# A fused attention and feed-forward kernel: the opening work of batches 0 and 1 is put in another order

## The chip, the cores and the metric

The kernel runs on one core of a Trainium2 chip. The metric is the device time of one execution in microseconds (us). Three executions of the kernel before took 340.25, 342.08 and 343.45 us, so their median is 342.08 us. Inputs and output are float32 in the chip's main memory; most arithmetic inside is float16, with float32 accumulation.

## The reference, cut to what matters

Eight batches of eight heads, 576 positions and 64 numbers per head go through an attention with two kinds of mask. The result is laid out as 4608 tokens of 512 numbers and goes through two matrix products with a leaky activation between them.

```python
scores = scale * np.matmul(q, k.transpose(0, 1, 3, 2))
rel = pos[:, None] - pos[None, :]
mask_local = (rel >= 0) & (rel < stride)                       # heads 0 to 3, stride 32
mask_strided = (rel >= 0) & (pos[None, :] % stride == pos[:, None] % stride)   # heads 4 to 7
scores = np.where(masks[None, :, :, :], scores, -1000000000.0)
attn = np.exp(scores - max);  attn = attn / sum(attn)
x = np.matmul(attn, v).transpose(0, 2, 1, 3).reshape(B * S, H * D)
h = x @ w_in                                                   # 512 -> 2048
g = np.maximum(h, 0.0) + alpha * np.minimum(h, 0.0)
out = g @ w_out                                                # 2048 -> 512
```

The kernel leaves out the subtraction of the maximum and gets each row's sum from a column of ones behind `v`.

## The kernel before, in words

Tokens are handled in nine chunks of 512. Layer 1 of a chunk makes `gT` (16 groups of 128 hidden units by 512 tokens): TensorE (PE) multiplies `win16` with the transposed attention result `xT`, ScalarE (ACT) writes the negative part into `neg`, VectorE (DVE) combines both into `gT`. Layer 2 multiplies `gT` with `wout16` and stores. Chunk 0 needs tokens 0 to 511 of batch 0; chunk 1 needs the last 64 tokens of batch 0 and most of batch 1.

Order is written out by hand. Every instruction goes through `keep`, so on each engine the instructions stand in the order in which the Python code issues them. An engine works its queue strictly in that order, and waits on semaphores where an input or a buffer isn't ready. The DMAs issued from GpSimd (POOL) stand in POOL's own queue among its copies and memsets; there are eight semaphores for them in turn, so each such DMA is issued only after the one eight places earlier has landed.

**Batch 0** is made in three parts of tokens (`pt` 0 and 1 with 256 tokens each, `pt` 2 with 64) by the functions named `dense_*`: `turn_s` and `turn_l` transpose q and k of the strided and of the local heads, `vcast` arranges v, `dense_s` and `dense_l` make scores and exponentials, `dense_pv` the weighted sums, `dense_x` the transposes into `xT`. In the kernel before, the first part runs alone; then layer 1 of chunk 0 starts on its tokens (`lin1_half(f, i)`: `f` is the half of the tokens, `i` one of eight pairs of hidden groups), the second part is put in as two blocks of five or six jobs after `lin1_half(0, 1)` and `lin1_half(0, 3)`, and the other twelve `lin1_half` follow without anything between them.

**Layer 2 of chunk 0** (L1181) is 48 matmuls of 512 columns: 16 values of `kf` for three banks of 128 tokens, in one run; the fourth group of tokens is made by four `lin2_piece` later. Then the third part of batch 0 runs, and then **batch 1** (`alone(3, 2)`): it has two units, 3 (the strided heads, pairs 6 and 7 of heads) and 2 (the local heads, pairs 4 and 5). `T(u, "q")` and `T(u, "k")` transpose a unit's q and k, `score_early` makes the scores of a pair and adds the mask to them by matmuls with an identity (L322), `Pv(g, a)` makes a third or a half of a pair's weighted sums, `X(g)` transposes them into `xT`. Chunk 1 starts after that (its first matmuls are those of L634), and from there on the attention of the next batch is put between the matmuls of a chunk.

**PSUM** has eight banks in three pools: `ps` (three one-bank buffers), `ph` (three, tag `hps`) and `pb` (one buffer of two banks, `sp`). The exponentials go to six buffers `et` in turn, 640 columns wide. The scores fill 576 of them. A `Pv` matmul takes 128 columns from its block's start, so that the last blocks also read columns 576 to 639, which are set to zero once (L1156, on DVE, between layer 1 and layer 2 of chunk 0).

**POOL's queue** is, in order: the loads of batch 0 and of `win16`; two tails, the last v rows of batch 0; four loads of `wout16` (`load_w(c, True)`); some memsets; unit 3 (`load_unit(1, True)`: q, k, tails, v) and unit 2 (`load_unit(1, False)`) of batch 1; q and k of batch 2's local heads (`load_qk`); the casts of batch 1 (`cast_v`, `cast_l`) and the copy `over_v` within v, with loads of batch 2 between and after them; `cast_l(2, ...)` last.

Of the kernel before, what the change touches and what calls it, by code (L numbers as in the profile page):

```python
# [41 lines left out]
def kernel(  # L42
# [10 lines left out]
    nc = tc.nc  # L53
# [333 lines left out]

    defer, defer_et = [], {}

    def score_both(P):  # L390

        w, r = P.w, 72 if P.strided else 128
        for i in range(2):
            et = ets[ectr["i"] % NE]
            ectr["i"] += 1
            if i:
                sps = [pspool.tile([128, 512], F32, tag="ps", name="sph") for _ in range(2)]
            else:
                sp = pbpool.tile([128, 2, 512], F32, tag="sp", name="sp")
                sps = [sp[:, y] for y in range(2)]  # L400
            grp = P.sgroups[i]
            n = w * len(grp)
            for x, t in enumerate(grp):
                if P.dx:
                    q0 = k0 = 80 * (4 * (2 * P.pr + t % 2) + t // 2)
                else:
                    q0, k0 = w * t, 32 + 72 * t if P.strided else 96 * t
                for y in range(2):
                    hf = slice(64 * y, 64 * y + 64)
                    keep(nc.tensor.matmul(  # L410
                        sps[y][:, w * x : w * x + w], P.kT[hf, k0 : k0 + 128],
                        P.qT[hf, q0 : q0 + w], start=(x == 0), stop=(x == len(grp) - 1),
                        skip_group_check=True))
                    P.et[(2 * (t // 2) + y, t % 2) if P.strided else (t, y)] = (et, n * y + w * x)
            ev = et[0:r, 0 : 2 * n]
            if not P.strided and i == 0:
                mv = ev.rearrange("r (y c) -> r y c", y=2)
                m = mfirst.unsqueeze(1).to_broadcast([r, 2, n])
            else:
                mv = ev.rearrange("r (c f) -> r c f", f=w)  # L420
                m = (mstr if P.strided else mother).unsqueeze(1).to_broadcast([r, 2 * n // w, w])
            if i == 0:
                keep(nc.scalar.activation(  # L423
                    ev.rearrange("r (y c) -> r y c", y=2), sp[0:r, :, 0:n], AF.Exp, scale=SCALE))
                keep(nc.gpsimd.tensor_tensor(mv, mv, m, op=ALU.mult))  # L425
# [487 lines left out]
    def dense_l(pt):  # L913

        b0, nb = 4 * pt, 4 if pt < 2 else 1
        nx = 2 if pt < 2 else 1
        sp = pbpool.tile([128, 2, 512], F32, tag="sp", name="sp")
        n = 192 * nx
        spv = sp[:, :, 0:n].rearrange("p e (y x c) -> p e y x c", y=2, x=nx)
        for e in range(2):  # L920
            fill(sp[:, e, 0:n], A["near"], 2 * nx, True)
        for e in range(2):
            hf = slice(64 * e, 64 * e + 64)
            for y in range(2):
                for kb in range(b0 - 1 if pt else 0, b0 + nb):
                    g = 64 * (kb % 2)
                    if kb < b0:
                        o, q0, w = spv[g : g + 64, e, y, nx - 1, 64:96], 64 * b0, 32
                    else:
                        w = 96 if kb < b0 + nb - 1 else 64  # L930
                        o, q0 = spv[g : g + 64, e, y, (kb - b0) // 2, 0:w], 64 * kb
# [3 lines left out]
        ed[("l", pt)] = [new_et()[:, 0:n] for _ in range(2)]  # L935
        for e in range(2):
            keep(nc.scalar.activation(ed[("l", pt)][e], sp[:, e, 0:n], AF.Exp, scale=SCALE))

    def dense_pv(kind, pt):

# [181 lines left out]
    dense_x("l", 0, "act")  # L1122
# [7 lines left out]
    keep(nc.vector.memset(qks["k"][64:80], 0.0))  # L1130
    keep(nc.vector.memset(x16s[64:80], 0.0))
    for i in range(2):
        keep(nc.gpsimd.memset(vls[i][0:32, 0:1, 0:64], 0.0))
        keep(nc.gpsimd.memset(vls[i][:, :, 64:65], 1.0))
        keep(nc.gpsimd.memset(vss[i][:, :, :, 64:65], 1.0))
    load_unit(1, True)
    load_unit(1, False)

    jobs = [
        lambda: turn_s("q", 1, "act"), lambda: turn_s("k", 1, "dve"),  # L1140
        lambda: dense_s(1), lambda: turn_l("q", 1, "act"), lambda: turn_l("k", 1, "dve"), lambda: vcast(1, "act"),
        lambda: dense_pv("s", 1), lambda: dense_l(1), lambda: dense_x("s", 1, ("act", "dve")),
        lambda: dense_pv("l", 1), lambda: dense_x("l", 1, "act")]
    for i in range(4):
        lin1_half(0, i)
        if i % 2:
            for _ in range(6):
                if jobs:
                    jobs.pop(0)()
    for f, i in ((1, 0), (1, 1), (1, 2), (1, 3), (0, 4), (0, 5), (1, 4), (1, 5), (0, 6), (0, 7), (1, 6), (1, 7)):  # L1150
        lin1_half(f, i)
    for i in range(2):
        keep(nc.vector.memset(kTs[i][:, :, 0:32], 0.0))
        keep(nc.vector.memset(kTs[i][:, :, 608:672], 0.0))
# [12 lines left out]
    load_d(2)  # L1167
    load_v(2, True)
# [3 lines left out]
    def attn_n(n, end):  # L1172
        for _ in range(n):
            attn_step(end)
        if n == 0:
            attn_step(0)

    banks = [phpool.tile([128, 512], F32, tag="hps", name="ops") for _ in range(3)]
    for kf in range(16):
        for mt in range(3):  # L1180
            keep(nc.tensor.matmul(  # L1181
                banks[mt], gTs[0][:, kf, 128 * mt : 128 * mt + 128], wout16[:, kf, :],
                start=(kf == 0), stop=(kf == 15)))
# [9 lines left out]
    dense_pv("s", 2)  # L1193
    dense_pv("l", 2)
    lin2_piece(0, 13)
    dense_x("s", 2, ("act", "dve"))
    dense_x("l", 2, "act")
    pos["i"] = end0
    for i in range(2):
        lin2_piece(0, 14 + i)  # L1200
        attn_step(end1)
        attn_step(end1)
    while pos["i"] < end1:
        attn_step(end1)
    wide["on"] = False
    load_unit(3, False)

# [58 lines left out]
```

## Time and profile before

| what | us |
|---|---|
| median of three executions | 342.08 |
| the profiled execution | 342.95 |
| its span, first to last instruction | 341.1 |
| opening, up to chunk 1's first matmul | 88.6 |
| chunks 1 to 8 | 252.5 |

The profile comes from one execution. It gives for each engine when an instruction ran, how long it was idle before it, and what ended that idle time. PEld is PE's loading of weights, which lies beside its matmuls. "PEclk" is the share of full clock that TensorE was granted. "L1181" is a line of the kernel before.

### The profile page before, as it was taken

The numbers are of one execution on the slowest core, as the hardware profiler recorded it, in microseconds if no ns is written. First come the engines' busy times: TensorE is split into PE (matmuls) and PEld (weight loads), VectorE is DVE, ScalarE is ACT, GpSimd is POOL, SyncE is SP. The second block draws the span as 40 slices with busy tenths as digits, with TensorE's granted clock in tenths as the row PEclk, the third lists the DMA queues.
The fourth block names the chain that finished last, engine by engine and source line by source line (L and its number), as shares of the span: only waits on it lengthen the run. The fifth ranks groups of instructions, "written<-read, shape, count | busy, mean of one in ns | idle before, by whom it ended". The sixth has DMA issues, their size and how long they took to land.

```text
span 341.1 us, 8353 instructions
## 1 busy us (share of the span) xinstructions
PE 317.3 (93%) x3436; PEld 211.0 (62%) x3436; DVE 219.7 (64%) x421; ACT 180.4 (53%) x335; POOL 174.3 (51%) x170
## 2 busy tenths in 40 slices
PE   8786989597899999999999999999999999999995
PEld 3564754356444544588778547854886776486484
DVE  3454561126578858875986689568847995864861
ACT  2242531126596557656755775577657626633740
POOL 7454577000359699749765774877372620400400
PEclk9787899969799999999999999999999999999999
DMA  8999999609904999749965992998071013003003
GB/s 188 210 201 206 237 170 114 143 1 213 197 1 54 137 161 234 95 67 208 206 67 98 258 153 25 160 152 98 19 171 50 20 32 112 0 2 126 0 2 123
DMA packets 81470, 40.18 MB, mean 118 GB/s; under 512 B 58440, under 2 KB 76728, under 8 KB 81432
## 3 DMA queue, kind: packets, MB, share of 16 engines
q0 software_dynamic: 41680, 16.76, 41.9%
q1 hardware_dynamic: 39608, 22.86, 29.3%
q8 instruction: 27, 0.44, 0.5%
q14 instruction: 11, 0.09, 0.1%
q10 hardware_dynamic: 144, 0.03, 0.0%
HBM read 38.15 MB, written 9.44 MB: 140 GB/s over the span
## 4 chain that ended last, share of the span: by engine, by line
PE 67%; DVE 15%; ACT 8%; issue 5%; DMA 2%; POOL 2%; SPq 0%; ACTq 0%; DVEq 0%
PE hps L634 23%; PE ops L761 19%; DVE gT L647 5%; PE hps L1059 5%; PE ops L675 4%; PE ops L1181 3%; DVE gsum L705 3%; PE pv L453 2%; ACT xT L492 2%; DVE x L462 2%; DMA madd_t<-consts 2%; ACT et L429 2%; PE sp L410 1%; ACT neg L644 1%; PE tp L250 1%
## 5 line engine op out<-in xcount | busy, mean ns | idle before, releaser
L634 PE MATMUL hps<-xT,win 128*128 128x512 f16 (+4 forms) x640 | 120.5, 339 | 0.6
L647 DVE SCALAR_TENSOR_TENSOR gT<-neg,oma,hps 128x512 f16<-128x512 f32 x128 | 93.6, 743 | 37.0 <-ACT neg L644 31.5
L644 ACT ACTIVATE neg<-hps 128x512 f32<-128x512 f32 x128 | 76.5, 598 | 35.5 <-PE hps L634 33.9
L634 PEld LDWEIGHTS <-win 128*128 128x128 f16 x640 | 56.9, 98 | 48.0 <-issue 3.2
L425 POOL TENSOR_TENSOR et<-et,consts 128x576 f16<-128x576 f16 (+1 forms) x24 | 30.7, 1278 | 58.4 <-ACT et L423 58.3
L705 POOL TENSOR_TENSOR gsum<-gT 128x1024 f16<-128x1024 f16 x14 | 29.7, 2129 | 40.5 <-DVE gT L647 40.5
L761 PEld LDWEIGHTS <-gsum 128*128 128x128 f16 x448 | 41.3, 98 | 7.6 <-DVE gsum L705 3.0
L761 PE MATMUL ops<-wsum,gsum 128*128 128x256 f16 x328 | 41.7, 273 | 1.0 <-DVE gsum L705 0.8
L761 PEld LDWEIGHTS <-gT 128*128 128x128 f16 x336 | 31.1, 98 | 6.8 <-DVE gT L647 1.6
L432 POOL TENSOR_TENSOR et<-et,consts 128x576 f16<-128x576 f16 (+1 forms) x24 | 30.9, 1286 | 0.6 <-ACT et L429 0.6
L761 PE MATMUL ops<-wout,gT 128*128 128x256 f16 x224 | 29.2, 273 | 0.5
L462 DVE TENSOR_TENSOR x<-pv,rc 96x384 f16<-96x384 f32 (+2 forms) x52 | 27.7, 533 | 1.8
L460 DVE RECIPROCAL rc<-pv 72x6 f32<-72x6 f32 (+2 forms) x70 | 12.8, 183 | 20.4 <-PE pv L453 20.3
L453 PEld LDWEIGHTS <-et 72*128 72x128 f16 (+1 forms) x392 | 20.6, 98 | 8.0 <-POOL et L432 0.8
L182 POOL DMA_DIRECT2D vl<-in_v_dram x7 | 10.1, 1437 | 28.1 <-PE pv L453 27.2
L423 ACT ACTIVATE et<-sp 128x576 f16<-128x576 f32 (+1 forms) x24 | 15.5, 646 | 12.9 <-PE sp L410 12.9
L675 PE MATMUL ops<-wout,gT 128*128 128x512 f16 x80 | 22.1, 404 | 0.0
L429 ACT ACTIVATE et<-sph 128x288 f16<-128x288 f32 (+1 forms) x48 | 18.4, 410 | 0.0
L1059 PE MATMUL hps<-xT,win 128*128 128x256 f16 x128 | 17.9, 302 | 0.5 <-ACT xT L190 0.5
L1067 DVE SCALAR_TENSOR_TENSOR gT<-neg,oma,hps 128x256 f16<-128x256 f32 x32 | 14.0, 478 | 6.6 <-ACT neg L1064 6.2
L778 ACT COPY par<-ops 128x512 f32<-128x512 f32 x13 | 7.6, 587 | 16.9 <-PE ops L761 16.9
L714 ACT COPY osb<-ops 128x512 f32<-128x512 f32 x14 | 8.2, 586 | 15.7 <-PE ops L761 15.7
(155 smaller groups left out, 423.6 us busy)
## 6 DMA issues: line engine op xcount, KB each, us to landing
out_dram<-osb SPq DMA_DIRECT2D x35, 256.0 KB, 3.0
ql<-in_q_dram SPq DMA_DIRECT2D x5, 512.0 KB, 4.1
kl<-in_k_dram SPq DMA_DIRECT2D x5, 512.0 KB, 6.9
vl<-in_v_dram POOLq DMA_DIRECT2D x6, 384.0 KB, 9.0
win<-in_moe_w_in_dram POOLq DMA_DIRECT2D x4, 512.0 KB, 10.8
wout<-in_moe_w_out_dram POOLq DMA_DIRECT2D x4, 512.0 KB, 12.9
stv<-in_v_dram POOLq DMA_DIRECT2D x7, 288.0 KB, 8.4
qsd<-in_q_dram POOLq DMA_DIRECT2D x6, 288.0 KB, 6.9
```

The costliest lines, as they stand in the source:

```text
L425: keep(nc.gpsimd.tensor_tensor(mv, mv, m, op=ALU.mult))
L429: keep(nc.scalar.activation(ev[:, n * y : n * y + n], sps[y][0:r, 0:n], AF.Exp, scale=SCALE))
L432: keep(nc.gpsimd.tensor_tensor(mv, mv, m, op=ALU.mult))
L453: keep(nc.tensor.matmul(pv[:, 65 * x : 65 * x + 65], et[0:r, c : c + 128], v16[0:r, 2 * P.pr + hh, t, :] if P.strided else v16[:, 6 * (2 * ...
L462: keep(nc.vector.tensor_tensor(P.x16[0:w, c0 : c0 + 64 * nb].rearrange("r (c e) -> r c e", e=64), pvv[:, :, 0:64], rc[0:w, 0:nb].unsqueeze ...
L634: keep(nc.tensor.matmul(hps[:, dst : dst + w], win16[:, kk, 128 * m : 128 * m + 128], xT[:, kk, src : src + w], start=(kk == 0 and x == 0) ...
L644: keep(nc.scalar.activation(neg, hps, AF.Relu, scale=-1.0))
L647: keep(nc.vector.scalar_tensor_tensor(gTs[n][:, m, :], neg, oma[:, m : m + 1], hps, op0=ALU.mult, op1=ALU.add))
L675: keep(nc.tensor.matmul(ops, gTs[n][:, kf, 128 * mt : 128 * mt + 128], wout16[:, kf, :], start=(kf == 0), stop=(kf == 15)))
L705: keep((nc.vector if eng == "dve" else nc.gpsimd).tensor_tensor(gsum[i][:, hs], a, b, op=op))
L761: keep(nc.tensor.matmul(o, lhs(y), rhs(y), start=(first and y == 0), stop=(y == 7), skip_group_check=True))
L1059: keep(nc.tensor.matmul(hps[:, 256 * j : 256 * j + 256], win16[:, kk, 128 * m : 128 * m + 128], xT[:, kk, 256 * f : 256 * f + 256], start= ...
```

## The change

- `score_both` gets a parameter `eng`. With it the mask is multiplied in after the exponentials by the engine named, with nothing put off; pairs 4 to 7 now use it with DVE, so that the mask matmuls of `score_early` go.
- `dense_l` takes one `ps` bank for each of its two halves in place of the two-bank buffer of `pb`.
- `turn_s` of the second part and `dense_s(1)` go in among the first part. The other eight jobs of the second part follow one by one behind the eight `lin1_half(0, i)`; the eight `lin1_half(1, i)` come after all of them.
- In layer 2 of chunk 0 the jobs of batch 1's strided heads (`T(3, ...)`, the scores and sums of pairs 6 and 7, `X(6)`) follow the values of `kf` from 5 on, one each. Batch 1's local heads are put between the third part of batch 0 and the four `lin2_piece`.
- Memsets go from DVE to POOL: those of `kT`, `qks` and `x16s` ahead of the loads of `wout16`, those of `et` behind `cast_l(2, ...)`.
- POOL loads the first two pieces of `wout16`, then unit 3, then the other two pieces, then unit 2, then the tails and last v rows of batch 0. `load_qk(2, ...)` comes behind the casts of batch 1.

```diff
-    def score_both(P):
+    def score_both(P, eng=None):
...
+            if eng is not None:
+                if i == 0:
+                    keep(nc.scalar.activation(
+                        ev.rearrange("r (y c) -> r y c", y=2), sp[0:r, :, 0:n], AF.Exp, scale=SCALE))
...
+                keep((nc.vector if eng == "dve" else nc.gpsimd).tensor_tensor(mv, mv, m, op=ALU.mult))
+                continue
...
-        sp = pbpool.tile([128, 2, 512], F32, tag="sp", name="sp")
...
         for e in range(2):
+            sp = pspool.tile([128, 512], F32, tag="ps", name="scl")
...
     dense_pv("s", 0)
+    turn_s("q", 1, "act")
     dense_l(0)
-    dense_x("s", 0, ("act", "dve"))
+    turn_s("k", 1, "act")
+    dense_x("s", 0, ("dve", "act"))
     dense_pv("l", 0)
...
+    dense_s(1)
+    dense_x("l", 0, "act")
...
-    load_tail(0, False)
-    first_vl(4, 64)
-    for c in range(4):
-        load_w(c, True)
-    keep(nc.vector.memset(qks["q"][64:80], 0.0))
...
+        keep(nc.gpsimd.memset(kTs[i][:, :, 608:672], 0.0))
+    for nm in "qk":
+        keep(nc.gpsimd.memset(qks[nm][64:80], 0.0))
+    keep(nc.gpsimd.memset(x16s[64:80], 0.0))
+    for c in range(2):
+        load_w(c, True)
     load_unit(1, True)
+    for c in range(2, 4):
+        load_w(c, True)
     load_unit(1, False)
+    load_tail(0, False)
+    first_vl(4, 64)
 
     jobs = [
...
+    for i in range(8):
         lin1_half(0, i)
+        jobs.pop(0)()
+    for i in range(8):
+        lin1_half(1, i)
...
-    for t in ets:
-        keep(nc.vector.memset(t[:, 576:640], 0.0))
-
-    load_qk(2, False, "q")
-    load_qk(2, False, "k")
     for pr in range(2):
         cast_v(1, pr, "pool")
     cast_l(1, "q")
-    load_tail(2, False)
     cast_l(1, "k")
     over_v(1, "pool")
+    load_qk(2, False, "q")
+    load_qk(2, False, "k")
+    load_tail(2, False)
     load_v(2, False)
     load_d(2)
     load_v(2, True)
     cast_l(2, "q")
     cast_l(2, "k")
...
+    jobs = [T(3, "q"), T(3, "k"), sc1(6), sc1(7), Pv(6, 0), Pv(6, 1), Pv(6, 2), Pv(7, 0), Pv(7, 1), X(6), Pv(7, 2)]
+    for t in ets:
+        keep(nc.gpsimd.memset(t[:, 576:640], 0.0))
     for kf in range(16):
         for mt in range(3):
             keep(nc.tensor.matmul(
                 banks[mt], gTs[0][:, kf, 128 * mt : 128 * mt + 128], wout16[:, kf, :],
                 start=(kf == 0), stop=(kf == 15)))
+        if kf >= 5:
+            jobs.pop(0)()
...
-    vcast(2, "dve")
-    rest_turn()
-    dense_s(2)
-    dense_l(2)
-    lin2_piece(0, 12)
...
+    jobs = [
+        T(2, "q"), T(2, "k"), X(7), lambda: lin2_piece(0, 12), sc1(4), rest_turn, sc1(5), lambda: lin2_piece(0, 13),
+        Pv(4, 0), Pv(4, 1), lambda: dense_s(2), lambda: vcast(2, "dve"), Pv(5, 0), X(4), lambda: dense_l(2),
+        Pv(5, 1), lambda: lin2_piece(0, 14), X(5),
+        lambda: dense_pv("s", 2), lambda: lin2_piece(0, 15), lambda: dense_pv("l", 2),
+        lambda: dense_x("s", 2, ("act", "dve")), lambda: dense_x("l", 2, "act")]
+    for fn in jobs:
+        fn()
```

More of the change, by code (lines that the diff above doesn't have):

```diff
@@ L421, in score_both @@
                 m = (mstr if P.strided else mother).unsqueeze(1).to_broadcast([r, 2 * n // w, w])
+            if eng is not None:
+                if i == 0:
+                    keep(nc.scalar.activation(
+                        ev.rearrange("r (y c) -> r y c", y=2), sp[0:r, :, 0:n], AF.Exp, scale=SCALE))
+                else:
+                    for y in range(2):
+                        keep(nc.scalar.activation(
+                            ev[:, n * y : n * y + n], sps[y][0:r, 0:n], AF.Exp, scale=SCALE))
+                keep((nc.vector if eng == "dve" else nc.gpsimd).tensor_tensor(mv, mv, m, op=ALU.mult))
+                continue
             if i == 0:
@@ L916, in dense_l @@
         nx = 2 if pt < 2 else 1
-        sp = pbpool.tile([128, 2, 512], F32, tag="sp", name="sp")
         n = 192 * nx
-        spv = sp[:, :, 0:n].rearrange("p e (y x c) -> p e y x c", y=2, x=nx)
+        ed[("l", pt)] = []
         for e in range(2):
-            fill(sp[:, e, 0:n], A["near"], 2 * nx, True)
-        for e in range(2):
+            sp = pspool.tile([128, 512], F32, tag="ps", name="scl")
+            spv = sp[:, 0:n].rearrange("p (y x c) -> p y x c", y=2, x=nx)
+            fill(sp[:, 0:n], A["near"], 2 * nx, True)
             hf = slice(64 * e, 64 * e + 64)
@@ L927, in dense_l @@
                     if kb < b0:
-                        o, q0, w = spv[g : g + 64, e, y, nx - 1, 64:96], 64 * b0, 32
+                        o, q0, w = spv[g : g + 64, y, nx - 1, 64:96], 64 * b0, 32
                     else:
                         w = 96 if kb < b0 + nb - 1 else 64
-                        o, q0 = spv[g : g + 64, e, y, (kb - b0) // 2, 0:w], 64 * kb
+                        o, q0 = spv[g : g + 64, y, (kb - b0) // 2, 0:w], 64 * kb
                     keep(nc.tensor.matmul(
@@ L934, in dense_l @@
                         start=False, stop=False, skip_group_check=True))
-        ed[("l", pt)] = [new_et()[:, 0:n] for _ in range(2)]
-        for e in range(2):
-            keep(nc.scalar.activation(ed[("l", pt)][e], sp[:, e, 0:n], AF.Exp, scale=SCALE))
+            et = new_et()[:, 0:n]
+            ed[("l", pt)].append(et)
+            keep(nc.scalar.activation(et, sp[:, 0:n], AF.Exp, scale=SCALE))
     def dense_pv(kind, pt):
@@ L1135 @@
         keep(nc.gpsimd.memset(vss[i][:, :, :, 64:65], 1.0))
+        keep(nc.gpsimd.memset(kTs[i][:, :, 0:32], 0.0))
+        keep(nc.gpsimd.memset(kTs[i][:, :, 608:672], 0.0))
[4 more added lines that the diff above has]
+        load_w(c, True)
     load_unit(1, True)
+    for c in range(2, 4):
+        load_w(c, True)
     load_unit(1, False)
+    load_tail(0, False)
+    first_vl(4, 64)
     jobs = [
-        lambda: turn_s("q", 1, "act"), lambda: turn_s("k", 1, "dve"),
-        lambda: dense_s(1), lambda: turn_l("q", 1, "act"), lambda: turn_l("k", 1, "dve"), lambda: vcast(1, "act"),
-        lambda: dense_pv("s", 1), lambda: dense_l(1), lambda: dense_x("s", 1, ("act", "dve")),
+        lambda: turn_l("q", 1, "act"), lambda: turn_l("k", 1, "act"), lambda: vcast(1, "dve"),
+        lambda: dense_pv("s", 1), lambda: dense_l(1), lambda: dense_x("s", 1, ("dve", "act")),
         lambda: dense_pv("l", 1), lambda: dense_x("l", 1, "act")]
-    for i in range(4):
+    for i in range(8):
         lin1_half(0, i)
[L1146 to L1154, printed above, removed]
-    for t in ets:
-        keep(nc.vector.memset(t[:, 576:640], 0.0))
-    load_qk(2, False, "q")
-    load_qk(2, False, "k")
+        jobs.pop(0)()
+    for i in range(8):
+        lin1_half(1, i)
     for pr in range(2):
@@ L1176, in attn_n, with sc1 @@
             attn_step(0)
+    def sc1(g):
+        return lambda: score_both(pairs[g], "dve")
+    jobs = [T(3, "q"), T(3, "k"), sc1(6), sc1(7), Pv(6, 0), Pv(6, 1), Pv(6, 2), Pv(7, 0), Pv(7, 1), X(6), Pv(7, 2)]
+    for t in ets:
+        keep(nc.gpsimd.memset(t[:, 576:640], 0.0))
     banks = [phpool.tile([128, 512], F32, tag="hps", name="ops") for _ in range(3)]
@@ L1187 @@
         keep(nc.sync.dma_start(out[128 * mt : 128 * mt + 128, :], osb))
-    vcast(2, "dve")
-    rest_turn()
-    dense_s(2)
-    dense_l(2)
-    lin2_piece(0, 12)
[L1193 to L1204, printed above, removed]
+    jobs = [
[6 more added lines that the diff above has]
+        fn()
+    pos["i"] = end1
     wide["on"] = False
```

3 lines of the change are left out of this document (removed).

## The prediction, made before the result was known

> **What bounds the kernel now.** I read first the page's span and chain, then the busy time by stage: the opening cut at layer 1's start, at the end of the second part, at layer 2, at the third part and at batch 1. Columns: length, busy time of PE, PEld, DVE, ACT, POOL with instructions, granted clock, DMA share, GB/s.
>
> ```profile
> span 341.1 us, 8353 instructions
> PE 67%; DVE 15%; ACT 8%; issue 5%; DMA 2%; POOL 2%; SPq 0%; ACTq 0%; DVEq 0%
> 17.00:34.80 17.80, 13.43 (x302) 10.09 (x300) 8.93 (x18) 6.94 (x13) 9.30 (x20) 0.79 1.29 204
> 34.80:48.40 13.60, 12.53 (x97) 9.46 (x97) 10.56 (x27) 7.17 (x12) 9.64 (x12) 0.91 1.57 211
> 48.40:58.40 10.00, 10.00 (x47) 4.38 (x47) 0.49 (x10) 0.33 (x1) 6.99 (x7) 1.00 1.10 122
> 58.40:72.60 14.20, 9.88 (x274) 5.88 (x273) 3.06 (x9) 3.09 (x10) 1.26 (x2) 0.83 0.51 100
> 72.60:88.60 16.00, 12.89 (x200) 9.61 (x199) 9.80 (x27) 10.02 (x23) 1.17 (x1) 0.93 0.66 166
> 88.60:341.10 252.50, 245.49 (x2319) 163.76 (x2317) 180.72 (x316) 148.87 (x270) 135.79 (x112) 0.99 0.61 99
> ```
>
> From 88.6 us on PE is busy for 245.5 of 252.5 us; nothing there is edited, so I carry it over unchanged. The opening has the room: layer 2 of chunk 0 keeps PE full while DVE and ACT idle (0.49 and 0.33 us in 10), and around it PE idles 4.4 us in the second part and 4.3 and 3.1 us in the last two stages. **The question is when chunk 1's first matmul can start**, 88.6 us now. The last stages also run below full clock:
>
> ```profile
> 66.28 0.29 PE L953 MATMUL pvd<-wsum,et 32*32 32x65 f16 x12 [1.81 <-issue]
> 68.00:70.00 2.00, 2.00 (x12) 0.79 (x11) 0.59 (x2) 0.00 (x0) 0.00 (x0) 0.50 0.00 0
> 72.00:74.00 2.00, 2.00 (x13) 1.28 (x12) 0.00 (x0) 0.00 (x0) 0.00 (x0) 0.50 0.00 0
> 74.00:76.00 2.00, 2.00 (x17) 1.15 (x15) 1.09 (x4) 1.15 (x4) 0.00 (x0) 0.83 0.00 0
> ```
>
> After idle PE time of 1.81 and 1.06 us at 64.5 to 67.6 the clock is at half from 68 to past 74, though PE has work throughout.
>
> **The change part by part. Up to layer 2: shorter, by about 6.5 us, and it doesn't count.** The eight jobs of the second part move between eight layer-1 pieces, so their waits find matmuls. What ends last then is DVE.
>
> ```profile
> 38.34 9.97 DVE L1067 SCALAR_TENSOR_TENSOR gT<-neg,oma,hps 128x256 f16<-128x256 f32 x22 [0.48 <-ACT neg L1064]
> 48.37 10.10 PE L1181 MATMUL ops<-wout,gT 128*128 128x512 f16 x46 [0.56 <-DVE gT L1067]
> ```
>
> One layer-1 piece costs DVE 2 x 0.453 = 0.91 us. DVE's busy time from 17 to 48.4 is 19.5 us, so layer 1 can't be done before some 36 us; 48.4 is the other end. I take 42: eight pieces with jobs at some 2 us each from 17.7, then eight at 0.94. Layer 2's matmuls come 0.22 us apart. With the 33 up to `kf` 10 and the transposes, scores and first `Pv` between, PE comes to `Pv(6, 1)` at about 52.
>
> **There it meets a new wait.** `Pv(6, 1)` reads columns above 576 of the first `et`; the memset of these stood on DVE and took 0.29 us for all six. Now it stands on POOL, behind `cast_l(2, "k")`. In the changed program the weight load of that `Pv` waits for POOL's memset of `et0`. Behind it in PE's queue stand the rest of layer 2 and all of batch 1. So I follow POOL's queue.
>
> ```profile
> 15.76 0.74 POOL L796 DMA_DIRECT2D win<-in_moe_w_in_dram  x1 [3.05 <-DMA win<-in_moe_w_in_dram]
> 26.23 0.70 POOL L125 DMA_DIRECT2D qs<-in_q_dram  x1 [1.06 <-DMA win<-in_moe_w_in_dram]
> 29.43 0.74 POOL L174 DMA_DIRECT2D stv<-in_v_dram  x1 [0.69 <-DMA wout<-in_moe_w_out_dram]
> 37.09 0.64 POOL L164 DMA_DIRECT2D tl<-in_q_dram  x1 [1.80 <-DMA wout<-in_moe_w_out_dram]
> 41.12 0.72 POOL L125 DMA_DIRECT2D ql<-in_q_dram  x1
> 41.84 0.73 POOL L125 DMA_DIRECT2D kl<-in_k_dram  x1
> 46.16 0.64 POOL L164 DMA_DIRECT2D tl<-in_k_dram  x1
> 49.77 1.43 POOL L194 COPY vl<-vl 32x1495 f16<-32x1495 f16 x1 [1.92 <-DMA vl<-in_v_dram]
> 51.15 1.45 POOL L182 DMA_DIRECT2D vl<-in_v_dram  x1
> ...
> 54.78 1.04 POOL L194 CAST ql<-ql 128x1024 f16<-128x1024 f32 x1
> 55.77 1.03 POOL L194 CAST kl<-kl 128x1024 f16<-128x1024 f32 x1
> stv<-in_v_dram POOLq DMA_DIRECT2D x1, 288.0 KB, 12.4
> 24.82 0.35 POOL L1135 MEMSET vs<- 128x32 f16 x1
> ql<-in_q_dram SPq DMA_DIRECT2D x5, 512.0 KB, 4.1
> ql<-in_q_dram POOLq DMA_DIRECT2D x2, 512.0 KB, 10.5
> ```
>
> Transfers are lined up without a gap here (DMA share above 1.2), so an order of loads changes when each lands and not when all have. The last piece of `wout` landed at 37.1, `stv` at 29.43 + 12.4 = 41.8: 4.7 us of unit 3 now go ahead of it, and the tails go behind, so `wout` is whole at about 41. Layer 2 asks for its third piece (`kf` 8) at about 49: **nothing to pay**. What lands before `over_v` is the same up to those small loads, so `over_v` runs again at about 49.3 to 50.7. Behind it POOL now first issues q and k (1.45 us), the tails (2 x 0.64), then the row's four loads from 51.15 to 54.78 (3.6), then does two casts (2.0): 50.7 + 8.3 = 59.0. The first memset is 0.1 to 0.35 us: **59.2**. Low bound 56.8, where the same casts ended before though their loads were issued 9 us earlier. High bound: q was issued at 50.7, and if it takes the 10.5 us of POOL's row, it lands at 61.2, and with both casts the memset starts at 63.4 or a little later. By the SP row of 4.1 us nothing waits. The 10.5 us stood behind megabytes of weights and now the line is nearly empty, so I take 59.2.
>
> The memsets that moved ahead of `wout`'s loads (no row shows POOL at that size) cost nothing while the line holds transfers: the last piece of `win` landed at 26.2, POOL came free at 16.5; that is cover for some 5 us of them, and beyond it 1:1 until the 7 us of slack before the new wait are gone.
>
> **DVE masks** have no row. Bounds are 0.38 us (576/1024 of a DVE product) and 1.28 (POOL's mask); I take 0.5, as it is the same engine. They hide beside `Pv` and matmuls, except the first two, which lie beside `over_v` on POOL. Whether DVE holds up POOL there no row shows (casts took 1.03 us beside a busy DVE and beside an idle one, but that DVE work read PSUM); between 0 and 1 us I put 0.3: PE goes on at **59.5**.
>
> ```profile
> L705 DVE TENSOR_TENSOR gsum<-gT,gsum 128x1024 f16<-128x1024 f16 x14 | 9.3, 680 | 0.0
> L425 POOL TENSOR_TENSOR et<-et,consts 128x576 f16<-128x576 f16 x12 | 15.4, 1281 | 32.3 <-ACT et L423 32.2
> 44.53 1.03 POOL L194 CAST ql<-ql 128x1024 f16<-128x1024 f32 x1
> ```
>
> (The Trainium skill, "SBUF — State Buffer", section "Who interferes with whom", says that a DVE instruction with two SBUF inputs contends with a GpSimd instruction that reads SBUF. The mask is one, `over_v` reads SBUF; by this rule two masks in the way would make my 0.3 into 1.0 and the time 0.7 us longer.)
>
> **From there to chunk 1.** PE's busy time from 58.4 to 88.6 was 9.88 + 12.89 = 22.8 us. What had been done by then: the transposes of unit 3 (2.1 us), the scores of pairs 6 and 7 (1.2). What is gone: the mask matmuls, 0.67 us in four places (2.7). What is new there: 15 matmuls of layer 2 (3.3).
>
> ```profile
> 73.03 1.06 PE L250 MATMUL tp<-ident_t,qs 128*128 128x128 f16 x8
> 74.80 0.29 PE L275 MATMUL tt<-ident_t,tl 64*128 64x64 f16 x4
> 76.14 0.30 PE L310 MATMUL sp<-qT,kT 64*128 64x72 f16 x8
> 76.51 0.42 PE L322 MATMUL sp<-madd_t,ident_t 72*128 72x288 f16 x2
> 76.77 0.41 PE L322 MATMUL sph<-madd_t,ident_t 72*128 72x288 f16 x2
> ```
>
> 22.8 - 2.1 - 1.2 - 2.7 + 3.3 = 20.1 us. This holds some 7 us at half clock; PE's idle 7 us before 59.5 should bring that again, so it stays. To it comes idle time: 7.4 us before (30.2 - 22.8), of which 1.8 the gap above. The jobs are now mixed, but three `ps` banks serve nearly all of them; I take 4.5, with 2 and 7.4 as ends. Chunk 1 starts at 59.5 + 20.1 + 4.5 = 84.1: **4.5 us earlier**, between 1.6 and 7.0. The profiled execution (342.95, span 341.1 and 1.85 around it) becomes 338.4; the median, 0.87 lower, 337.6. I say **338.0**.
>
> (The Trainium skill, "TensorE: Matmul & The Clock Gate", section "Part 1: The HAM clock gate", has the clock back after about 3.4 us of sustained work. The trace disagrees here: 0.50 for over 6 us of busy PE. By the page the half-clock stretch would cost some 1.7 us less, and the time be 336.3.)
>
> **The rivals.**
> - *The wait costs nothing*, as if POOL reached the memset by 52. Then PE goes on 7.5 us earlier and without the half clock (3.5 us of its 7): 338.0 - 11.0 = 327. Against it: even with the older, earlier issues the casts ended at 56.8. 4%.
> - *The wait is longer*: k of batch 2 lands late, the memset is at 63.4. Then 338.0 + 4.2 = 342: the mixing is eaten whole, the change doesn't do what it says. For it: POOL's row of 10.5. 16%.
> - *Slower, by the `ps` ring*: from the end of layer 2 to chunk 1, 22 jobs take a bank from three; before, four score banks came from `hps`. If each waits for a reader, at an exponential's or a copy's length, as here:
>
> ```profile
> 67.63 0.28 PE L945 MATMUL pvd<-wrm 128*128 128x260 f16 x1 [1.06 <-DVE x L979]
> 77.66 0.31 PE L310 MATMUL sp<-qT,kT 64*128 64x72 f16 x8 [0.49 <-ACT et L325]
> ```
>
>   then at 0.6 us each the idle time is 13 us, and chunk 1 starts at 92.6: 346.5. From 0.41 us each (9.0 us idle, start 88.6) the gain is gone. Against it: PE's order puts a long matmul group or another unit's job between most bank users. 17%.
>
> **How the numbers follow.** My forecast (334.5 to 341) has 56%, the free wait 4, the late wait 16, the bank ring 17, and 7 for what I don't see, spread over all. One per cent, 3.4 us, is about what tells from no change: below 338.7 is faster. Of my forecast two thirds lie there (0.37), with the free wait and a part of the rest 0.46; the same: 0.19 + 0.13 of the late wait and 0.02, 0.34; slower 0.20. The range must leave out no more than a fifth: the free wait and the worse half of the bank ring fall outside, so 333.5 to 345.
>
> **What would show it.** In the profile after: PE idle before `pv` for some 7 us, ended by POOL, at 52 to 59.5 (right), or no idle time over 1 us there (wrong). POOL without pause from `over_v` to six memsets of `et`, first at 59.2. Layer 1's last `gT` at 42 instead of 48.3. Clock 0.5 for several us after that wait. Chunk 1's first layer-1 matmul at 84. Many waits of `xp`, `tp`, `sph` on ACT or DVE over 0.4 us between 68 and 84 would be the ring. I am wrong if chunk 1 itself changes its 252.5 us, for instance by a clock that starts lower.

## The result, and the profile after

The kernel after takes **338.2 us** (median of 18 runs, 335.11 to 341.36) against 341.98 us of before in the same rounds (339.28 to 343.53): ratio 0.988, 95% interval 0.985 to 0.9915, about 4 us less. (Medians and ranges are of all runs; ratios and intervals leave out the runs that are more than 1.5% longer than the fastest of their kernel.) The profiled execution is the longest of the 18 (341.36 us, span 339.6), so places and lengths are read from it and totals from the medians.

The waits of PE from layer 2 to chunk 1 in the profile after (total, times, longest, in us):

```profile
PE pv L463 <- POOL et L1191: 8.0, 1, 8.0
PE xp L480 <- ACT qT L190: 1.4, 1, 1.4
PE ops L1195 <- DVE gT L1077: 1.0, 2, 0.6
```

One wait stands out, and it is the new one: `Pv(6, 1)` (L463) for POOL's memset of `et` (L1191). Where it lies, in PE's timeline of the same kernel (start, length, engine, line, what; in brackets the idle time before it and what ended it):

```profile
43.54 3.63 PE L1195 MATMUL ops<-wout,gT 128*128 128x512 f16 x16 [0.49 <-DVE gT L1077]
...
60.91 0.46 PE L463 MATMUL pv<-vs,et 72*128 72x65 f16 x5 [7.98 <-POOL et L1191]
...
84.75 1.89 PE L644 MATMUL hps<-xT,win 128*128 128x512 f16 x8 [0.35 <-ACT xT L190]
```

Layer 2 runs in earnest from 43.5 us (48.4 before), and chunk 1 starts at 84.75 (88.6 before). The 4.8 us gained by layer 2 go into this wait, which takes 8.0. POOL's timeline says why it ends at 60.9:

```profile
18.31 1.80 POOL L1145 MEMSET qsd<- 16x2048 f16 x1
20.06 1.80 POOL L1145 MEMSET ksd<- 16x2048 f16 x1
21.81 0.94 POOL L1146 MEMSET x16s<- 16x1024 f16 x1
22.70 1.48 POOL L802 DMA_DIRECT2D wout<-in_moe_w_out_dram  x2
...
50.93 1.52 POOL L194 COPY vl<-vl 32x1495 f16<-32x1495 f16 x1 [1.75 <-DMA vl<-in_v_dram]
52.41 0.73 POOL L125 DMA_DIRECT2D ql<-in_q_dram  x1
...
58.74 1.04 POOL L194 CAST ql<-ql 128x1024 f16<-128x1024 f32 x1
59.72 1.03 POOL L194 CAST kl<-kl 128x1024 f16<-128x1024 f32 x1
60.70 0.57 POOL L1191 MEMSET et<- 128x64 f16 x6
```

From `over_v`'s copy at 50.93 to the memsets POOL doesn't pause: copy, eight issues, two casts, 9.8 us. The casts follow the last issue at once, so the loads of batch 2 were there in time. The copy came 1.2 us later than before (49.77), and the first load of `wout` 4.4 us later (22.70 against 18.33), behind three memsets of 4.5 us together.

The stretches of the kernel after: the wait, what follows it, all from the wait's end to chunk 1, and chunks 1 to 8 (columns as in the prediction):

```profile
52.00:61.00 9.00, 1.02 (x13) 0.47 (x11) 2.16 (x5) 0.40 (x2) 8.96 (x15) 0.73 1.20 176
61.00:67.00 6.00, 6.00 (x39) 2.97 (x40) 2.84 (x8) 0.00 (x0) 1.49 (x6) 0.55 1.10 150
60.90:84.75 23.85, 20.03 (x412) 12.37 (x413) 12.84 (x35) 9.29 (x23) 4.29 (x10) 0.88 0.63 88
84.75:339.60 254.85, 244.43 (x2316) 163.44 (x2315) 180.12 (x315) 148.53 (x270) 134.20 (x109) 1.00 0.62 107
```

PE is busy for 1 us of the first nine, then for six without pause at a clock of 0.55. From the wait's end to chunk 1 there are 20.0 us of PE work and 3.8 of idle time. Chunks 1 to 8 hold 244.4 us of PE work, as before (245.5). They are 2.4 us longer in this execution; in it one output transfer, from 181.56 us on, took 6.2 us to land and held up a buffer.

### The profile page after: what moved, and what is told of

It reads as the page before. It is cut to its first block, busy times and chain, and to the rows that moved or that the text cites. A ratio compares the mean times of both kernels' runs of the same rounds, so it can differ in the third digit from the quotient of the medians.

```text
span 339.6 us, 8324 instructions
## 1 busy us (share of the span) xinstructions
PE 310.5 (91%) x3420; PEld 206.0 (61%) x3420; DVE 220.5 (65%) x415; ACT 180.3 (53%) x336; POOL 179.6 (53%) x183
## 4 chain that ended last, share of the span: by engine, by line
PE 52%; DMA 14%; DVE 13%; POOL 8%; ACT 7%; issue 6%; DVEq 0%; ACTq 0%; POOLq 0%
PE hps L644 21%; PE ops L771 18%; DVE gT L657 5%; DMA vl<-in_v_dram 4%; PE ops L685 3%; DMA win<-in_moe_w_in_dram 3%; DMA ks<-in_k_dram 3%; DMA out_dram<-osb 3%; PE pv L463 2%; DVE gsum L715 2%; DVE x L472 2%; ACT neg L654 2%; PE ops L1195 2%; ACT xT L502 2%; ACT et L439 2%
## 5 line engine op out<-in xcount | busy, mean ns | idle before, releaser
L644 PE MATMUL hps<-xT,win 128*128 128x512 f16 (+4 forms) x640 | 119.3, 337 | 2.7 <-ACT osb L724 1.6
L644 PEld LDWEIGHTS <-win 128*128 128x128 f16 x640 | 56.6, 98 | 49.5 <-issue 3.7
L463 PEld LDWEIGHTS <-et 72*128 72x128 f16 (+1 forms) x392 | 21.5, 100 | 18.2 <-POOL et L1191 8.3
L463 PE MATMUL pv<-vs,et 72*128 72x65 f16 x224 | 14.6, 199 | 8.1 <-POOL et L1191 8.0
L1077 DVE SCALAR_TENSOR_TENSOR gT<-neg,oma,hps 128x256 f16<-128x256 f32 x32 | 13.9, 477 | 10.8 <-ACT neg L1074 10.7
L685 PE MATMUL ops<-wout,gT 128*128 128x512 f16 x80 | 20.4, 380 | 0.0
L1069 PE MATMUL hps<-xT,win 128*128 128x256 f16 x128 | 17.1, 285 | 1.1 <-ACT xT L190 1.1
```

The lines of the kernel that those rows point to most:

```text
L463: keep(nc.tensor.matmul(pv[:, 65 * x : 65 * x + 65], et[0:r, c : c + 128], v16[0:r, 2 * P.pr + hh, t, :] if P.strided else v16[:, 6 * (2 * ...
L644: keep(nc.tensor.matmul(hps[:, dst : dst + w], win16[:, kk, 128 * m : 128 * m + 128], xT[:, kk, src : src + w], start=(kk == 0 and x == 0) ...
L685: keep(nc.tensor.matmul(ops, gTs[n][:, kf, 128 * mt : 128 * mt + 128], wout16[:, kf, :], start=(kf == 0), stop=(kf == 15)))
L1069: keep(nc.tensor.matmul(hps[:, 256 * j : 256 * j + 256], win16[:, kk, 128 * m : 128 * m + 128], xT[:, kk, 256 * f : 256 * f + 256], start= ...
```

## The experiments

**The memset of `et` on DVE (e1_et_dve).** The kernel after with only this moved:

```
     for i in range(8):
         lin1_half(1, i)
+    for t in ets:
+        keep(nc.vector.memset(t[:, 576:640], 0.0))
...
-    for t in ets:
-        keep(nc.gpsimd.memset(t[:, 576:640], 0.0))
```

> The changed kernel with the six memsets of et back on DVE, right behind layer 1; all else as changed. Theory (the wait for POOL's memsets, 8.0 us in the profile after, holds the rest of the opening one for one, and the half clock of about 5.5 us behind it costs another 2.7): PE goes on at about 52.8, chunk 1's first matmul comes at about 74 in place of 84.75, time about 327.5 us (325.5 to 330). Rival 1 (the bank ring of ps or the loads are next at once behind the wait): chunk 1 not before 80, time 334 to 338. Rival 2 (the wait hides other waiting, such as DVE's masks, of the same length): time within 1 us of 338.2.

Measured: 330.43 us (328.75 to 332.18), ratio to before 0.965 (0.959 to 0.971). Its stretches from layer 2's first matmul to chunk 1's (at 73.96) and from there to the end:

```profile
41.58:73.96 32.38, 27.52 (x506) 16.21 (x504) 19.36 (x55) 13.61 (x34) 18.25 (x21) 1.00 1.36 146
74.00:326.80 252.80, 244.38 (x2316) 163.44 (x2315) 180.11 (x315) 148.52 (x270) 134.21 (x109) 1.00 0.63 108
```

Chunk 1 starts at 74.0, where the theory put it, 10.8 us earlier than in the kernel after; the clock is 1.00 throughout. The median fell by 7.8, less than the 10.8 of the two profiles, and lies just above the expected range: the profiled execution of after is 3.2 us above its median and this one 1.7 below. The one wait takes back more than half of what the change wins: without it the gain on before is nearly 12 us in place of 4.

**The memset earlier in POOL's queue (e2_et_pool_earlier)**, ahead of the two casts of batch 2 and of nothing else:

```
     load_v(2, True)
+    for t in ets:
+        keep(nc.gpsimd.memset(t[:, 576:640], 0.0))
     cast_l(2, "q")
```

> The changed kernel with the six memsets of et still on POOL, but ahead of the two casts of batch 2 in its queue, which take 2.0 us. Theory (each us of POOL's queue ahead of the memset is a us of the whole): the wait ends at 58.8 in place of 60.9, time 338.2 - 2.0 = 336.2 us (335.2 to 337.2). Rival 1 (another wait lies just below): no change, 338.2.

Measured: 337.62 us (337.0 to 339.23), ratio 0.985 (0.98 to 0.99). POOL's timeline of it:

```profile
58.26 0.62 POOL L1178 MEMSET et<- 128x64 f16 x6
```

The memset comes 2.4 us earlier and chunk 1 at 82.7 in place of 84.75, in the direction and about the size expected. The median is only 0.6 us lower and lies between the expected range and the rival's number; the interval (some 1.7 us to either side) can't tell 0.6 from 2.

**The old order of transfers (e3_old_loads).** Both parts of it, unit 3's loads behind all four of `wout`, and batch 2's q and k issued ahead of batch 1's casts:

```
-    for c in range(2):
+    load_tail(0, False)
+    first_vl(4, 64)
+    for c in range(4):
         load_w(c, True)
     load_unit(1, True)
-    for c in range(2, 4):
-        load_w(c, True)
     load_unit(1, False)
-    load_tail(0, False)
-    first_vl(4, 64)
...
+    load_qk(2, False, "q")
+    load_qk(2, False, "k")
     for pr in range(2):
         cast_v(1, pr, "pool")
```

(`load_tail(2, False)` goes back between the two casts, the two `load_qk` behind `over_v` go.)

> The changed kernel with POOL's transfers in the old order: tails and last v rows of batch 0, four pieces of wout, unit 3, unit 2, and q and k of batch 2 issued ahead of the casts of batch 1. Memsets stay where the change put them. Theory (the new order buys nothing for layer 2 and, by issuing q and k of batch 2 behind over_v, lengthens POOL's queue ahead of the memset of et): the memset comes at 58 to 59 in place of 60.7, time 335 to 336.5 us. Rival (the new order is what lets unit 3 run within layer 2): PE then waits for unit 3's q, k or v before it reaches the memset, time 338.5 or more.

Measured: 336.75 us (335.45 to 342.27), ratio 0.982 (0.976 to 0.988). The wait's end, on POOL and on PE:

```profile
56.78 0.57 POOL L1189 MEMSET et<- 128x64 f16 x6
```

```profile
57.00 0.46 PE L463 MATMUL pv<-vs,et 72*128 72x65 f16 x5 [6.57 <-POOL et L1189]
```

The memset of `et` comes at 56.8 in place of 60.7, earlier than the 58 to 59 expected: POOL has 2.7 us less to issue between `over_v` and the casts, and `over_v` itself starts 1.3 us earlier (49.63). PE still waits 6.6 us for it, because layer 2 began 2.5 us earlier in this execution. PE reaches the memset without waiting for unit 3's loads, so the rival doesn't hold. The median lies 0.25 us above the theory's range, and its interval overlaps that of the kernel after.

**The first part alone (e4_first_part).** The kernel before with the second part of batch 0 spread over layer 1 (its `turn_s` and `dense_s(1)` among the first part, as in the change) and the one-bank local scores; batch 1, the memsets and the transfers stay as they were:

```
-    for i in range(4):
+    for i in range(8):
         lin1_half(0, i)
-        if i % 2:
-            for _ in range(6):
-                if jobs:
-                    jobs.pop(0)()
-    for f, i in ((1, 0), (1, 1), ... (1, 6), (1, 7)):
-        lin1_half(f, i)
+        jobs.pop(0)()
+    for i in range(8):
+        lin1_half(1, i)
```

> The kernel before with the first part of the change alone: second part of batch 0 spread over layer 1, strided transposes and scores ahead of it, one-bank local scores. Batch 1, transfers, memsets and mask matmuls as before. Theory (what the spread gains, layer 1 done at about 43.5 in place of 48.3, is swallowed by the new wait in the changed kernel, but isn't here): 342.0 - 4.8 = 337.2 us (336 to 338.5), so this half alone gives as much as the whole change. Rival (the gain of the change comes from batch 1's new place): 340.5 to 342.

Measured: 336.73 us (335.44 to 338.69), ratio 0.984 (0.978 to 0.989): as much as the whole change. So the rest of the change (batch 1 spread over layer 2, the masks on DVE, the moved memsets and the order of the loads) brings nothing on top as it stands; e1 shows some 6 us in it (336.7 to 330.4) once the wait is gone. In the profile of e4 PE pauses for 4.64 us at 57 to 61.6 us, for which no releaser shows, so no price of a single stage is read from it.

**PE kept busy through the wait (e5_warm_wait).** The wait stays, but 34 matmuls whose result nobody reads stand ahead of it:

```
+        if kf == 10:
+            wp = pbpool.tile([128, 2, 512], F32, tag="sp", name="wp")
+            for _ in range(34):
+                keep(nc.tensor.matmul(wp[:, 0], wrm[:, 0:128], wrm, start=True, stop=True))
         if kf >= 5:
             jobs.pop(0)()
```

> The changed kernel with 34 idle matmuls (512 columns each, result unused) ahead of Pv(6, 1), so PE has work for most of the 8 us in which it waits for the memset; the wait itself stays. Theory (the wait costs twice: its own length, and then the half clock, 6 us of busy PE at 0.50 to 0.55 behind it): the memset of et stays at about 60.7, the clock is 1.00 at 61 to 67, chunk 1 starts some 2.7 us earlier, at about 82; 335.5 us (334.5 to 337). Rival (the half clock doesn't matter, since what stands behind the wait is bound by DVE and ACT): same as the changed kernel, 338.2, chunk 1 at 84 to 85.

Measured: **334.75 us** (334.54 to 335.23), ratio 0.978 (0.974 to 0.982), below that of after without overlap. POOL's timeline, and the stretch from the wait's end to chunk 1, which starts at 81.97:

```profile
60.57 0.57 POOL L1191 MEMSET et<- 128x64 f16 x6
```

```profile
60.75:81.97 21.22, 17.38 (x411) 11.31 (x412) 12.84 (x35) 9.29 (x23) 4.31 (x10) 1.00 0.71 100
```

The memset comes when it came (60.57 against 60.70), and yet chunk 1 starts 2.8 us earlier. The same 411 or 412 matmuls recorded take 17.38 us in place of 20.03, while idle time stays at 3.8. So in the profiles the wait costs twice: 8.0 us itself, and 2.65 for the clock it leaves behind. In the medians the clock is worth 3.4 us (338.2 to 334.75) and the wait itself only 4.3 (334.75 to e1's 330.43); the profiled execution here is the slowest of its six and that of e1 the fastest of its four, and where the rest of the 8.0 goes no run tells. The six runs lie within 0.7 us of each other, the 18 of after spread over 6; that the clock does this isn't shown, as e1 and e7, which have no half clock behind 21.4 us in their profiles, spread over 3.4 and 8.8.

**The memsets of `qks` and `x16s` back on DVE (e6_memsets_dve):**

```
     for nm in "qk":
-        keep(nc.gpsimd.memset(qks[nm][64:80], 0.0))
-    keep(nc.gpsimd.memset(x16s[64:80], 0.0))
+        keep(nc.vector.memset(qks[nm][64:80], 0.0))
+    keep(nc.vector.memset(x16s[64:80], 0.0))
```

> The changed kernel with the three memsets of qks and x16s back on DVE; the order of the transfers is that of the changed kernel. They took POOL 4.5 us ahead of wout's first load. Theory (POOL issues wout's first load 4.4 us late, the line of transfers runs dry for about 1.5 us, everything behind it lands that much later, and so the memset of et comes 1.4 us late): first load of wout issued at about 18.3, the wait on et ends at 59.3 to 59.6, chunk 1 at about 83.3; 336.8 us (336 to 337.7). Rival (the transfers hide the 4.5 us, and the wait is late for another reason): wait ends at 60.5 to 61, 338.2.

Measured: 337.92 us (336.9 to 341.12), ratio 0.988 (0.983 to 0.993). POOL's timeline of this kernel, then the transfers (last column, GB/s) in the same two stretches of it and of the kernel after:

```profile
17.65 1.49 POOL L802 DMA_DIRECT2D wout<-in_moe_w_out_dram  x2
...
59.16 0.58 POOL L1191 MEMSET et<- 128x64 f16 x6
```

```profile
22.00:24.00 2.00, 2.00 (x19) 1.63 (x17) 1.03 (x3) 1.14 (x2) 0.29 (x1) 1.00 1.25 207
24.00:26.00 2.00, 1.19 (x68) 0.89 (x67) 1.96 (x6) 0.60 (x1) 0.44 (x1) 1.00 1.24 209
```

```profile
22.00:24.00 2.00, 2.00 (x27) 1.68 (x28) 0.87 (x2) 1.31 (x3) 2.00 (x3) 0.98 0.92 154
24.00:26.00 2.00, 1.22 (x11) 0.83 (x10) 1.50 (x4) 1.06 (x2) 2.00 (x4) 1.00 0.83 107
```

Chunk 1 starts at 82.48 in this profile (83.3 expected). In the kernel after the line of transfers runs thin from 22 to 26 us, 154 and 107 GB/s in place of 207 and 209: 0.31 MB less, 1.5 us of the full rate. With the memsets on DVE the line stays full, and the memset of `et` starts 1.54 us earlier. The trace agrees with the theory; the median, 0.3 us below that of after and outside the expected range, doesn't show it. The next pair asks the same without the half clock behind the wait.

**The same two, with the clock kept up (e10_warm26 and e9_warm_memsets).** Both have the idle matmuls of e5, 26 of them; e9 has the three memsets on DVE as well.

> e5_warm_wait with 26 idle matmuls in place of 34, so that they end some 2 us before the memset of et and PE's wait ends with the memset in every execution. It is the base for e9_warm_memsets. Theory (the half clock is gone as long as PE idles less than one step of 3.4 us; the wait's end is set by POOL): 334.8 us (334.3 to 335.5), the wait on et ends at 60.5 to 61, clock 1.00 throughout. Rival (the clock falls in the idle rest): 336 to 338.

> e10_warm26 with the three memsets of qks and x16s on DVE (the edit of e6_memsets_dve), where no half clock behind the wait spreads the times. Theory (the late wout loads leave a gap in the transfers, and the wait on et ends 1.5 us late for it): wait ends at 59.2 to 59.5, 1.5 us below e10_warm26: 333.3 us (332.7 to 334). Rival (the 1.5 us of e6_memsets_dve were only the scatter of where the opening starts): as e10_warm26, 334.8.

Measured: e10 334.82 us (334.37 to 335.95), ratio 0.979 (0.975 to 0.983); e9 **332.36 us** (331.77 to 334.34), ratio 0.972 (0.969 to 0.976). POOL's timeline of e10, then of e9:

```profile
21.23 1.48 POOL L802 DMA_DIRECT2D wout<-in_moe_w_out_dram  x2
...
59.66 0.57 POOL L1191 MEMSET et<- 128x64 f16 x6
```

```profile
17.24 1.49 POOL L802 DMA_DIRECT2D wout<-in_moe_w_out_dram  x2
...
57.40 0.58 POOL L1191 MEMSET et<- 128x64 f16 x6
```

Layer 2 starts at 40.1 and 40.2 us in the two, and the memset of `et` 2.3 us earlier in e9; the medians are 2.5 us apart, more than the 1.5 expected. No run of e9 is as long as the shortest of e10, so the memsets on POOL do cost, and the thin stretch of the transfers is the way that the traces show. The start of `over_v` says the same in more profiles: 49.2 to 50.9 us in the six kernels with these memsets on POOL and the loads in the order of after (after, e1, e2, e5, e8, e10), 47.7 to 49.5 in the three with them on DVE (e6, e7, e9). One pair of profiles alone wouldn't do, since the six differ by 1.7 among themselves. The rival of e10 was partly right too: in its profiled execution (335.72 us) the clock did fall for 3.4 us, though PE had idled only 3.0.

**The masks on PE again (e8_mask_pe)**, on top of e1: `sc1` calls `score_early`, whose `sph` tiles come from `ps` for it.

```
-        return lambda: score_both(pairs[g], "dve")
+        return lambda: score_early(pairs[g])
```

> e1_et_dve with the masks of units 3 and 2 in the opening back on PE (the matmuls of madd, 0.67 us at each of four pairs) in place of DVE's products; one score group's banks are then held until its mask matmuls are through. Theory (PE is the bound behind layer 1, the 2.7 us of mask matmuls were on the path): 330.4 + 2.7 = 333.1 us (332 to 334), chunk 1 at 76.7. Rival (they fall into PE's idle time of 3.8 us between 43.5 and 74): 330.4 to 331.

Measured: 330.08 us (328.04 to 330.49), ratio 0.963 (0.959 to 0.967), near the rival's 330.4 to 331. Its stretch from layer 2's first matmul to chunk 1, and one row of its PE timeline:

```profile
40.63:75.69 35.06, 29.39 (x521) 17.89 (x520) 15.75 (x47) 13.79 (x34) 18.25 (x21) 1.00 1.29 151
```

```profile
74.95 0.23 PE L1015 MATMUL xpd<-ident_t,x 32*64 32x32 f16 x4 [1.63 <-issue]
```

The stretch is 2.7 us longer than in e1 (32.38): 1.9 more of PE work, a pause of 1.63 us for which no releaser shows, and 0.8 less of other idle time. Yet the median is that of e1. The profile sides with the theory, the times with the rival; what the masks on DVE are worth stays open.

**The best version run (e7_best):** e1 with the memsets of e6, and a piece of layer 2 moved into the wait of `xp`:

```
-        T(2, "q"), T(2, "k"), X(7), lambda: lin2_piece(0, 12), sc1(4), rest_turn, ...
+        T(2, "q"), T(2, "k"), lambda: lin2_piece(0, 12), X(7), sc1(4), rest_turn, ...
```

> The memset of et on DVE behind layer 1 (as in e1_et_dve), the three memsets of qks and x16s on DVE too, and lin2_piece(0, 12) ahead of X(7), so that 1.0 us of matmuls stands in the 1.45 us in which xp waits for ACT's eviction. Theory: only the moved piece pays, 1.0 us less than e1_et_dve (330.4): 329.5 us (328.5 to 330.5), chunk 1 at about 73. Rival (what stands behind, on DVE and ACT, is the bound there, or the transfers still are): 330.4 to 331, the wait returns at the next bank user.

Measured: **327.99 us** (324.88 to 333.64), ratio 0.954 (0.948 to 0.960), faster than both kernels and below the expected range. Its runs overlap those of e1, so what it gains over e1 isn't shown. Its waits of PE, and the stretch from layer 2 to chunk 1:

```profile
PE ops L1195 <- DVE gT L1077: 1.0, 2, 0.6
...
PE xp L480 <- ACT qT L190: 0.6, 1, 0.6
```

```profile
40.03:71.73 31.70, 27.64 (x505) 16.51 (x504) 18.79 (x55) 13.53 (x34) 18.25 (x21) 1.00 1.35 140
```

The wait of `xp` shrinks from 1.4 to 0.6 us and the stretch by 0.7, less than the 1.0 expected. The rest of the 2.2 us by which chunk 1 is earlier than in e1 (73.96 to 71.73) lies ahead of layer 2's start (41.58 to 40.03); how much of that the memsets brought and how much is scatter, one profile doesn't tell.

## Why the prediction was right

338.0 us was predicted and 338.2 measured. The mechanism is the one that was named, shown by e1 and e5. That the number is as near as this is luck: the sum itself gave 337.6 for the median, the places below come from an execution 3.2 us above its median, and terms that were each off by more than 0.6 us nearly cancel: the start of chunk 1, 84.1 predicted and 84.75 measured, has 1.4 us more for the wait's end, 0.8 more for PE work at full clock, 0.85 less for the half clock and 0.7 less idle time.

- **Up to layer 2, shorter by 6.5 us and not counting.** Layer 1 was done at 43.5 rather than 42, PE stood at `Pv(6, 1)` at 52.9 rather than 52. That it doesn't count is right: the 4.8 us gained went into the wait of 8.0 us. In e4, which has no such wait, the same step alone gives the whole gain.
- **The new wait.** Right in place, in its releaser and in its queue. It ended at 60.9, not 59.5: 1.4 us too early in the sum. The 8.3 us from `over_v`'s end to the memset were right (52.45 to 60.70 is 8.25); the start of `over_v` was late by 1.6, and the 0.3 put in for DVE against POOL was 0.09.
- **The moved memsets "cost nothing".** This is the step that failed. I knew no row of POOL's memset at that size and gave it 5 us of cover; the memsets took 4.5 us, and the transfers ran thin all the same. The cover was counted to the moment at which the last `win` piece lands. But here the line was thin earlier; the e6 profile shows 207 GB/s where the kernel after has 154. Priced by e6 and e9: 1.5 to 2.3 us later at the memset of `et`, enough for the 1.6 above. (`wout` was whole at 43.8 us, not 41: POOL's issue at 43.84 waits for its last piece. No wait of layer 2 for it shows, so the "nothing to pay" for the order of the loads holds.)
- **Batch 2's loads.** The choice of SP's 4.1 us against POOL's 10.5 was right in its effect: q was issued at 52.41 and had landed by 58.74, where its cast begins, and both casts followed the last issue without a pause. The rival of 342 falls with it.
- **DVE's masks.** 0.5 us was taken; DVE's rows in the kernel after, the first two masks one after the other:

```profile
50.70 0.46 DVE L430 TENSOR_TENSOR et<-et,consts 72x576 f16<-72x576 f16 x1 [0.53 <-ACT et L424]
51.30 1.47 DVE L430 TENSOR_TENSOR et<-et,consts 72x576 f16<-72x576 f16 x1
```

  The first took 0.46. The second began when POOL's copy of `over_v` was already running (50.93 to 52.45) and took 1.47, ending 0.3 us after the copy. The other two, which began behind the copy, took 0.44 to 0.46 again. So it was DVE that lost to POOL, by 1.0 us, and not POOL to DVE: the copy itself took 1.52 us against 1.43 before. The prediction's 0.3 for POOL was too much, and the loser of the pair was taken wrongly. (The Trainium skill, "SBUF — State Buffer", section "Who interferes with whom", says that the shared port goes to whichever issued first and that the other blocks; this trace agrees.) PE, which waited until 60.9 anyway, lost nothing by it.
- **From the wait to chunk 1.** Predicted 20.1 us of PE work and 4.5 idle; measured 20.03 and 3.82. The work agrees only in sum: at full clock it is 17.4 us (e5), where the prediction had 20.1 less 3.5, so 16.6; and the half clock cost 2.65, not 3.5.
- **The clock.** The sum carried over some 7 us at half clock; 5.5 came. The prediction found that the trace speaks against the Trainium skill ("TensorE: Matmul & The Clock Gate", section "Part 1: The HAM clock gate"), because 0.50 lasted for over 6 us of busy PE. For that stretch of the kernel before this stands, and no run tells why; it is the one of 18 that doesn't fit, as the last section shows.
- **Chunks 1 to 8 unchanged.** In the profiles of all runs they take 250.8 to 254.9 us where 252.5 was carried over, with the same PE work within 2 us. That scatter is larger than several terms of the sum.
- **The rivals.** The free wait was put at 327; with the wait gone e1 measures 330.4, and its profile's gain, 10.8 us, is near the 11.0 that the rival named. The ring of `ps` banks doesn't show: PE idles 3.8 us in all between 60.9 and 84.75, and no wait there is longer than 1.45.

## What to carry to other kernels

Before a small operation is moved to another engine's queue, look at what stands ahead of it there and who waits for it: 0.57 us of memsets behind eight DMA issues and two casts held the busiest engine for 8 us and took most of the change back. A queue that issues DMAs should be free before the line of transfers runs thin: here 4.4 us of delay at an issue came out as 1.5 to 2.3 us at the end of the line, though earlier loads were still under way. And where an idle stretch of PE can't be avoided, matmuls that nobody reads can keep the clock up, and so what follows keeps its length; here 34 of them were worth 3.4 us, while with 26 the clock fell in the profile of e10.

## What the runs showed of the hardware that was not expected

**The granted clock changes in steps of 3.4 us.** Stretches of 0.1 us (clock third from the end) at which it falls and returns, of before (two pairs), of the kernel after, and of e6:

```profile
67.80:67.90 0.10, 0.10 (x2) 0.06 (x2) 0.00 (x0) 0.00 (x0) 0.00 (x0) 0.68 0.00 0
74.60:74.70 0.10, 0.10 (x4) 0.07 (x1) 0.10 (x1) 0.00 (x0) 0.00 (x0) 0.69 0.00 0
88.30:88.40 0.10, 0.00 (x0) 0.00 (x1) 0.05 (x1) 0.10 (x1) 0.10 (x1) 0.58 1.04 389
91.70:91.80 0.10, 0.10 (x1) 0.00 (x0) 0.10 (x1) 0.00 (x0) 0.00 (x0) 0.85 2.58 154
```

```profile
56.10:56.20 0.10, 0.00 (x0) 0.00 (x0) 0.00 (x0) 0.00 (x0) 0.10 (x1) 0.98 0.70 287
66.40:66.50 0.10, 0.10 (x2) 0.06 (x1) 0.10 (x1) 0.00 (x0) 0.00 (x0) 0.81 0.92 90
```

```profile
56.50:56.60 0.10, 0.00 (x0) 0.00 (x0) 0.00 (x0) 0.00 (x0) 0.10 (x1) 0.92 1.50 96
63.40:63.50 0.10, 0.10 (x1) 0.00 (x0) 0.10 (x1) 0.00 (x0) 0.00 (x0) 0.94 1.66 108
```

In these stretches PE stays at half clock for 6.8 and 3.4 us in before, 10.2 in after, 6.8 in e6; likewise 6.8 behind the wait in e2 and e3, 6.8 in e4 and 3.4 in e10: one, two or three times 3.4. With those of the first 40 us the twelve profiles hold 18 falls ahead of PE's last work, each of such a length. Cut each profile into steps of 3.4 us from the fall on. In 17 of the 18 the clock comes back at the end of the first step in which PE idles for less than 0.4 us; steps with 0.5 us or more of idle time didn't bring it back. In after PE resumes at 60.91 and the steps begin at 59.6 and 63.0, so the first is lost and the clock is back at 66.4, 5.5 us after the wait. In e6 it resumes at 59.37, just ahead of the step at 60.0, and the clock is back at 63.4, 4.0 us after. So the same wait costs 2 us or nearly 3 at half clock by where it ends in a step, which no term of a sum can foresee. That is too little for the 6 us over which the runs of after spread. (The Trainium skill, on the page and in the section named above, has a free-running window of 3.4 us; the lengths in the traces agree.)

The exception is the first pair above, the stretch that the prediction read. PE is busy without a pause from the fall at 67.8 on, also in the row between those that the prediction shows, and yet the clock comes back after two steps and not after one:

```profile
70.00:72.00 2.00, 2.00 (x37) 1.16 (x37) 0.23 (x1) 0.48 (x2) 0.00 (x0) 0.50 0.00 0
```

So busy time in the profile isn't all that decides, and what else does stays open. The same holds for the fall: the steps ahead of the 18 falls have 0.9 to 3.4 us of idle time, while other steps with up to 1.5 us left the clock up.

**Memsets on POOL are long for the few bytes they write:** 1.80 us for 16 x 2048 elements of two bytes and 0.94 for 16 x 1024 (rows above); the time follows the length of a row. DVE, in e6's timeline, writes the same bytes in half the time, as half as many elements of four bytes:

```profile
15.89 0.91 DVE L1145 MEMSET qsd<- 16x1024 uint32 x1 [0.27 <-DVE oma L1135]
17.93 0.48 DVE L1146 MEMSET x16s<- 16x512 uint32 x1
```

Per element the two engines are alike here, 0.9 ns; moving these memsets doubled their length, since on POOL they kept their two-byte elements.
